# A new hand-over list of steps for a one-core kernel that mixes an S5 scan and a Hedgehog linear attention

## The chip, the core and the metric

One core of a Trainium2 chip. Engines with a queue of instructions each: PE (TensorE, matrix products into PSUM), PEld (its weight loads), DVE (VectorE), ACT (ScalarE), POOL (GpSimd), and SP (SyncE), which here only issues DMAs. The metric is the device time of one execution in microseconds, lower is better.

## The reference, cut to what matters

`x` is 2048 x 512, bfloat16. Branch A is a diagonal complex state-space scan over the 2048 positions with 512 states; branch B is linear attention with 32 heads of width 16, whose features are softmaxes of a small projection and of its negative. A gate per position mixes them.

```python
g = sigmoid((x * gate_w).sum(-1, keepdims=True))
# A: h[t] = Lam_bar * h[t-1] + x[t] @ B_bar.T ; a = 2 * Re(h @ C.T) + x * Dskip
# B: q, k, v = heads of x @ wqkv; phi(u) = [softmax(u @ w_phi), softmax(-u @ w_phi)]
#    b = (phi(q) @ (phi(k).T @ v)) / (phi(q) @ phi(k).sum(0) + 1e-6) @ wo
out = g * a + (1 - g) * b
```

## The kernel before, in words

Positions are cut into 16 tiles of 128 rows. In the scan's layout row `c*8 + r` belongs to residue `r`, so tiles `2r` and `2r+1` hold residue `r`. The work is a set of generators, one for each piece; each `next` of a generator is one step and emits a few instructions for one or two engines. The string `ORDER` names the steps one after the other, and this order is the order of the instructions in the queues of PE, DVE, ACT and SP: nothing is reordered later, and only semaphores hold an instruction back. In a token, `@b` gives the PSUM banks that the step opens (eight banks, 0 to 7), `:D` puts a copy out of PSUM (or an absolute value) on DVE instead of ACT, `:A` issues an output DMA from ACT instead of SP, and `F:n` emits n matrix products whose result nobody reads. A bank is free again when its copy out of PSUM is done.

Before the list, SP issues `w_phi`, the transposing loads of x tiles 0 to 3 (line 229), the 512 KB of `Wv`, and x tiles 4 to 7; ACT issues the two halves of the k weights (line 165). The steps that the text speaks of:

- `NR`, `NI` (line 284): loads of the two 512 KB halves, real and imaginary, of A's matrix B; `l8` to `l15`: x tiles 8 to 15; `R0` to `R7` (line 288): transposes of B on the DMA queue, which wait for both halves; `Q`, `C`, `J`: loads for q's weights and A's matrix C; `O` (line 305): the 512 KB of `wo`. All are issued by SP.
- `W0` to `W3` (PE transposes of the k weights, line 274, then a copy), `f0` to `f3` (products that fold `w_phi` into them, line 431, then a copy; `fj` needs `Wj`), `V`, `P`, `P2`, `P3`, `P4`, `U`, `i0` to `i3`, `M`, `D`: scalars and tables of the scan; `M` runs on POOL, and `D` on DVE needs it. `L` pins an ACT table.
- `k0` to `k15`, `v0` to `v15`, `q0` to `q15` (line 475): four products of 512 columns and a copy out of PSUM. `kn` and `vn` need x tile n.
- For each group of k tiles (2, 2, 4, 4, 4 of them) `x` and `n` (maximum, minimum, line 511, then the differences, lines 521 and 527, DVE), `e` (exponentials, ACT), `s` (sums, DVE; logarithm, ACT; last a product, line 548, DVE) and `a` (the kv sums, PE, lines 578 and 582, into two banks held to the end; step `Y` reads them out, and `G` makes the gate). For the four groups of q tiles the same work is `xA`, `nA`, `eA`, `sA` and `X`, `N`, `E`, `S` with 1 to 3; there the last product (line 559) is followed by four DMA transposes (line 563) into `phT`, one per tile.
- `g` with r and j (lines 601 to 608): input of residue r for two of the eight state tiles, with a copy; `z0` to `z3`: the scan on DVE (line 641); `h` with r and j (line 668): states of the other residues, twenty of them added up on DVE (line 672); `c0` to `c7` (lines 590 and 594): scaled C matrices, with scratch space in `phT` of the first q group.
- For each output tile n: `y` (line 717, states times C, 512 columns; line 722, the skip term), `o` (line 736: numerator and denominator in two halves, on ACT a logarithm and a copy each, then an exponential; line 744 a product on DVE; then a DMA transpose, line 758, or for n = 12 to 15 a PE transpose, line 753, and a copy), `t` (line 765: times `wo`, onto y's bank; line 769 or 771 the gate; line 773 the output DMA). `o` of tile n needs transpose n of its group.

The list was written by a planner outside of the kernel that holds costs and landing times; of it the kernel has only the list.

Of the kernel before, what the change touches and what calls it, by code (L numbers as in the profile page):

```python
# [20 lines left out]
P = 128  # L21
MAGIC = 12582912.0
Z_MAX = 70.0
ORDER = """
B F:28 l11 F:4 W1@0 W0@1 W2@2 W1:D f1@3 W3@4 f1 W0:D f0@5 f0 NR W2:D f2@6 W3:D f3@0 f3 f2:D V@1 V P P P P2 P2 P2 P2 P2
P4 U P3 P4 P4 i1 i2 U l12 i1 i2 U F:4 k0@2 k0 NI P2 P3 l10 i0 l9 k1@3 k1 x0 i1 i1 i0 i2 k3@4 l14 x0 k2@5 n0 U M i1 k2
V2@6 v3@1 i2 x0 i0 v0@7 i0:D i0 v2@0 x0 k3 l8 n0 l13 i3 x0 k5@2 k5 i3 k4@3 v0 R0 x1 k6@5 n0 n0 i3 i3:D x1 x1 i2 k4 n0
v1@4 i3 L V2 k7@2 k7 n1 n1 x1 n1 gw x1 n1 R1 v6@7 e0 e0 v1 k6:D v4@6 n1 x2 n2 v7@3 v7 k11@2 v6 s0 x2 s0 e1 n2 s0 v5@5
v5 s0 s0 R2 D k12@4 R3 k10@3 k9@7 v4 k8@5 n2 l15 s0 e1 k13@6 v2 s1 k10 k14@0 s0 k11 C1 Q2 k8 C4 g20@3 s1 x2 k13 a0@25
k14 a0 n2 s1 k12 g20 x2 g00@6 k9 g30@0 s1 s1 s1 x2 n2 s1 v3 g40@4 x3 g01@3 g10@7 n3 R5 g00 a1 a1 x3 g60@1 n3 e2 R4  # L30
g11@6 g10 x3 g01 n3 e2 x3 e2 e2 n3 g11 k15@3 g60 g10 g30 g40 x3 s2 n3 g70@1 k15 g11 s2 x4 s2 s2 n4 g30 Q1 Q3 x4 n4 e3
e3 x4 C5 n4 Q0 x4 g50@7 g50 g50 s2 g21@4 n4 g21 s2 s2 v8@3 e3 e3 s3 g70 g70 g70 z0 s3 z0 g31@6 g31 s3 z0 z0 v11@0
g41@7 a2 C6 a2 g41 z0 z0 v11 g61@4 a2 g61 C7 w0@1 w0 C3 w1@7 w1 g31 a2 w2@0 w2 w3@4 s3 s3 g51@1 g51 g51 z0 R7 z0 x4
g62@7 w3 z0 z0 g71@6 g71 g02@0 v8 n4 s3 J2 g71 g71 z1 g02 z1 h50@1 h50 J2 z1 e4 e4 q1@4 h10@3 g62 g12@6 h10 g22@0 q2@1
z1 z1 z1 g22 q2 s3 z1 z1 q1 e4 h60@3 h60 g12 g12 z1 q3@7 q0@0 q0 q3 g32@1 e4 xA C2 g42@4 g32 nA g32 s4 g42 v9@6 v9 z1
s4 C0 J0 J0 g52@0 g52 c4 g52 nA c4 xA c4 R6 g72@7 g72 J1 s4 nA g23@3 g43@1 g03@4 g63@6 g72 g72 z2 h51@0 J3 c5 a3 g23
z2 J1 v10@7 h11@3 nA a3 c2 c2 g03 xA z2 z2 z2 z2 c0 h51 h61@4 z2 z2 g13@0 v10 xA h11 g43 c3 g13 a3 a3 J3 c5 z2 s4
g33@7 g13 g33 c0 z2 s4 s4 g33 h32@1 c2 h32 xA g53@3 g63 h52@0 g53 g53 nA s4 h52 h42@7 h42 eA c5 eA v14@1 v14 g73@6 g73
g73 q5@3 g73 h61 h12@0 h12 v12@1 v15@7 z3 z3 c0 z3 v12 eA eA h21@4 z3 v13@6 h21 a4 z3 z3 sA v13 z3 z3 c3 q10@0 q10
q6@1 v15 sA c1 c1 q4@4 q4 q6 a4 a4 c3 a4 h20@6 h30@0 h30 c7 q8@7 q12@4 q8 Y Y sA z3 z3 h33@2 q5 sA sA c1 h62@1 h20  # L40
h02@0 h33 sA sA q7@7 h62 G h43@3 h53@6 h02 c7 h13@2 Y Y sA q7 y6@1 h13 h01@0 h53 q12 c7 sA sA c6 q14@5 q14 h23@7 h23
h22@4 h31@2 h00@6 c6 q13@5 h31 h41@7 h43 c6 h22 h40@3 h63@2 h00 h41 h63 h40 h03@6 h03 sA sA y3@4 y3 END X1 o0@7 N1 X1
q13 o0 o0@2 O o0 N1 X1 q9@6 q9 N1 o1@3 X1 o1 o1@5 q11@7 o0 N1 X1 N1 o3@2 o1 o3 q11 X2 o1 o1 h01 X2 N2 X2 o3@6 o3 N2 X2
N2 E1 E1 E1 o1 E1 o0 o0 X2 S1 S1 N2 y0@3 o2@5 y0 y0 o2 o2@2 y3 o2 o2 y1@7 y1 S1 o3 o3 o3 S1 G y2@0 N2 q15@6 q15 S1 S1
o2 y1 o2 t1 S1 S1 G G y9@5 y9 E2 E2 y4@2 y4 y2 N3 E2 E2 y5@6 y9 y5 t1 S1 S1 S1 S1 X3 t3 t3 y2 t2 t2 X3 N3 N3 S2 X3 S2
t0 o4@7 y5 o4 o4@4 o4 N3 o4 X3 S2 y4 t0 y13@0 S2 o4 o5@7 o5 o5@4 o5 o5 y6 o4 y6 o6@3 S2 o6 o6@7 o6 X3 o5 y7@4 y7 o5 S2
S2 o7@3 N3 y13 o6 t4 t0:A o6 o6 E3 E3 E3 S2 S2 y8@7 t4:D o7:D E3 S3 t5 S2 S2 S2 t5 y12@2 S3 S3 o7@3 o7 o7 o7 t6 t6
o8@6 o8 o8@3 o8 o7 y12 y8 S3 t1:A o8 o8 o9@1 o9 o9@6 o8 y11@3 y11 S3 S3 y10@1 o9 o9 o9 S3 S3 t4:A o11@6 y7 t7 y12 o9
o11 t7 o10@6 y8 t8 t8 y11 y13 o11@4 t9 S3 S3 S3 o10 o11 S3 o10@7 t9:D y15@6 y14@4 o11 o11 o10 o10 t8:A o12@7 o12 o12@5
o12:D y15 o10 o12 o12 o11 o13@7 o13 o13@5 o13 o13 t2 y14 y14 o10 o12@7 t7:A t5:A o12:D o14@5 o14:D t3:A y10 o15@7 t9:A  # L50
y10 o15 o15@5 o15:D o15 o13 t12 o15 o14@7 o14 o14 t12:D t12 t11 t11:D o15@5 o15 o13@7 t10 t6:A t11 y15 o13:D t10 t10
t15 t15 t15:A o14 o14@2 t13 o14:D t13 t13 t14 t14 t14:A
"""
H_VECTOR = tuple((r, j) for r in (1, 2, 4, 5, 6) for j in range(4))
OT_PE = (12, 13, 14, 15)
# [792 lines left out]
```

## Time and profile before

| what | us |
|---|---|
| median of 3 runs (lowest to highest) | 156.41 (155.97 to 156.71) |
| the profiled execution | 156.63 |
| its span in the profile | 154.6 |
| busy PE, DVE, ACT, POOL | 147.7, 131.8, 129.4, 16.1 |
| first product on PE, last product's group begins | 1.11, 149.11 |
| queue q1 (SP's DMAs), share of 16 DMA engines | 53.2% of the span |

All times below count from the start of the span. A row in order of time gives start, length, engine, line, operation, result and operands, and the number of instructions merged; the bracket gives the idle time before it and what ended that. In rows of SP the length is that of issuing, and a separate view gives the time from issue to landing.

### The profile page before, as it was taken

How to read it: one execution, taken by the hardware profiler on the slowest of the kernel's cores; microseconds unless marked ns; L12 is line 12 of the kernel's file. 1: busy time of each engine (PE TensorE's matmuls, PEld its weight loads, DVE VectorE, ACT ScalarE, POOL GpSimd, SP SyncE). 2: the span in 40 equal slices, each digit the busy share in tenths (PEclk: the TensorE clock that was granted, in tenths of full speed). 3: DMA queues.
4: the chain of work that ended last, by engine and by line, in shares of the span. 5: the costliest groups of instructions: out<-in, count | busy, mean ns of one | idle time of the engine just before them, and what ended most of it. 6: DMA issues, size and time to landing. Idle time of an engine off the chain costs nothing.

```text
span 154.6 us, 3382 instructions
## 1 busy us (share of the span) xinstructions
PE 147.7 (96%) x1254; PEld 95.6 (62%) x1254; DVE 131.8 (85%) x303; ACT 129.4 (84%) x279; POOL 16.1 (10%) x43
## 2 busy tenths in 40 slices
PE   7999999999999999999999999999998999989990
PEld 7844444797789876888755767454454545545540
DVE  3789999999999999999999999999997966423730
ACT  3489999999999999999999996799497998465652
POOL 8239980000000000000000000000000000000000
PEclk9999999999999999999999999999999999999999
DMA  4785998465475849910000006943169689789742
GB/s 120 158 222 87 168 191 170 89 98 107 97 78 105 174 94 168 184 25 6 0 0 4 0 0 136 141 136 68 34 123 143 117 163 197 150 137 200 208 147 94
DMA packets 50848, 17.55 MB, mean 113 GB/s; under 512 B 44176, under 2 KB 50832, under 8 KB 50832
## 3 DMA queue, kind: packets, MB, share of 16 engines
q1 hardware_dynamic: 48544, 15.36, 53.2%
q10 hardware_dynamic: 2128, 1.97, 4.5%
q8 instruction: 10, 0.16, 0.4%
q14 instruction: 6, 0.05, 0.1%
q0 software_dynamic: 160, 0.01, 0.1%
HBM read 2.64 MB, written 2.10 MB: 31 GB/s over the span
## 4 chain that ended last, share of the span: by engine, by line
DVE 47%; PE 32%; DMA 8%; ACT 6%; issue 4%; DVEq 0%; SPq 0%
PE py L717 9%; DVE smk L511 6%; PE pk L475 6%; DMA oT<-on 5%; PE py L765 5%; PE pgq L601 4%; DMA phT<-EEq 3%; DVE Bn L672 3%; DVE EEk L548 3%; DVE w L641 3%; DVE HM L672 3%; DVE H L652 3%; PE spin L812 3%; DVE EEk L527 2%; DVE EEk L521 2%
## 5 line engine op out<-in xcount | busy, mean ns | idle before, releaser
L601 PE MATMUL pgq<-xT,BT 128*128 128x256 bf16 x256 | 31.2, 272 | 0.0
L475 PEld LDWEIGHTS <-xT 128*128 128x128 bf16 x192 | 18.3, 98 | 18.6 <-DMA xT<-in_A_x_dram 0.8
L601 PEld LDWEIGHTS <-BT 128*128 128x128 bf16 x256 | 24.7, 98 | 3.9
L138 ACT ACTIVATE EEk<-EEk 128x1024 bf16<-128x1024 bf16 x20 | 20.6, 1075 | 0.3 <-DVE EEk L527 0.3
L765 PE MATMUL py<-Wo,oT 128*128 128x512 bf16 x64 | 16.1, 379 | 0.9 <-DMA oT<-on 0.9
L119 ACT CAST uv<-pgq 128x512 bf16<-128x512 f32 x28 | 16.3, 604 | 0.3
L475 PE MATMUL pq<-Wq,xT 128*128 128x512 bf16 x64 | 15.8, 379 | 0.0
L475 PE MATMUL pv<-Wv,xT 128*128 128x512 bf16 x64 | 15.6, 379 | 0.0
L475 PE MATMUL pk<-Wk,xT 128*128 128x512 bf16 x64 | 15.0, 379 | 0.3 <-ACT EEk L138 0.3
L138 ACT ACTIVATE ld<-pn 128x16 f32<-128x16 f32 x32 | 6.2, 193 | 7.6 <-PE pn L736 7.4
L138 ACT ACTIVATE EEq<-EEq 128x1024 bf16<-128x1024 bf16 x12 | 11.8, 1061 | 0.3 <-DVE EEq L527 0.3
L590 ACT ACTIVATE phT<-X,dgB 128x512 bf16<-128x512 bf16 x16 | 11.5, 740 | 0.0
L769 ACT ACTIVATE ot<-py,G 128x512 bf16<-128x512 f32 x12 | 8.0, 684 | 3.5 <-PE py L765 3.3
L119 ACT CAST nu<-pn 128x256 bf16<-128x256 f32 x28 | 10.3, 381 | 0.0
L736 PEld LDWEIGHTS <-phT 128*128 128x128 bf16 x128 | 6.7, 98 | 5.3 <-DMA phT<-EEq 1.2
L765 PEld LDWEIGHTS <-oT 128*128 128x128 bf16 x64 | 5.6, 97 | 6.2 <-DMA oT<-on 1.2
L119 ACT CAST vx<-pv 128x512 bf16<-128x512 f32 x16 | 9.4, 600 | 0.0
L548 DVE TENSOR_TENSOR EEk<-EEk,rck 128x4096 bf16<-128x4096 bf16 (+1 forms) x5 | 9.3, 1859 | 0.0
L119 ACT CAST Xq<-pq 128x512 bf16<-128x512 f32 x16 | 9.1, 610 | 0.2
L736 PE MATMUL pn<-KVm,phT 128*128 128x68 bf16 x128 | 8.0, 194 | 0.8 <-DMA phT<-EEq 0.7
L119 ACT CAST Xq<-pk 128x512 bf16<-128x512 f32 x15 | 8.4, 618 | 0.4 <-PE pk L475 0.4
L511 DVE TENSOR_TENSOR smk<-smk 128x512 bf16<-128x512 bf16 (+4 forms) x18 | 8.6, 476 | 0.1
(177 smaller groups left out, 319.6 us busy)
## 6 DMA issues: line engine op xcount, KB each, us to landing
X<-HM SPq DMA_DIRECT2D x8, 256.0 KB, 4.0
out_dram<-ot ACTq DMA_DIRECT2D x11, 128.0 KB, 2.5
out_dram<-ot SPq DMA_DIRECT2D x5, 128.0 KB, 2.5
C2r<-in_B_wqkv_dram ACTq DMA_DIRECT2D x2, 256.0 KB, 3.3
Wv<-in_B_wqkv_dram SPq DMA_DIRECT2D x1, 512.0 KB, 4.0
Bn<-in_A_B_re_dram SPq DMA_DIRECT2D x1, 512.0 KB, 5.5
Bn<-in_A_B_im_dram SPq DMA_DIRECT2D x1, 512.0 KB, 6.7
Wo<-in_B_wo_dram SPq DMA_DIRECT2D x1, 512.0 KB, 4.6
```

What stands on the lines that cost most here:

```text
L119: nc.scalar.copy(out=out_ap, in_=in_ap)
L138: ins = nc.scalar.activation(**kw)
L475: MM(out=pt[:], lhsT=xT[:, kt, ti * P:(ti + 1) * P], rhs=W[:, kt, :], start=(kt == 0), stop=(kt == KT - 1))
L511: VT(out=dst, in0=cur[:, :, :, 0:n, :], in1=cur[:, :, :, n:2 * n, :], op=op)
L548: VT(out=E5, in0=E5, in1=rc.to_broadcast([P, L, 2 * NB, Dh, 4]), op=ALU.mult)
L590: nc.scalar.mul(out=t_, in_=x_, mul=c_)
L601: MM(out=pg[:, h, :], lhsT=BT[:, kt, 2 * j + h, :], rhs=xT[:, kt, r * NC:(r + 1) * NC], start=(h == 0 and kt == 0), stop=(r % 2 == 0 and k ...
L672: VT(out=dst, in0=ph[:], in1=uv[j][:, r], op=ALU.add)
L717: MM(out=py[:], lhsT=hs(r, t, slice(a * P, (a + 1) * P)), rhs=C2B[t], start=(t == 0), stop=False)
L736: MM(out=pn[:, 4 * m:4 * m + 4, :].rearrange("p h e -> p (h e)"), lhsT=ph[:, 4 * hf + m, :], rhs=KVm[:, 4 * hf + m, :], start=(m == 0), st ...
L765: MM(out=py[:], lhsT=oT[:, g, :], rhs=Wo[:, g, :], start=False, stop=(g == HG - 1))
L769: nc.scalar.mul(out=ot[:], in_=py[:], mul=G[:, ti:ti + 1])
```

## The change

The string `ORDER` is replaced; nothing else is touched. Both lists have 855 tokens and the same steps. Their order and banks differ, and so do some marks: `W0` and `W3` are copied by ACT instead of DVE, `f1` by DVE instead of ACT; `i2` and `i3` change engines for the absolute value; `o7`, `o9`, `o11`, `o12`, `o15`, `t7`, `t10`, `t11`, `t12` and `o13` differ in some copies, and outputs go 8 times through ACT instead of 11. `NR` and `NI` now stand first, ahead of all of `l8` to `l15`; before, `l11` stood ahead of both and `l12` between them. Two groups of four fills moved from before `W1` and before `k0` to behind `V` and `f3`. The sums use banks 7 and 1 instead of 2 and 5. The diff, cut:

```diff
 ORDER = """
-B F:28 l11 F:4 W1@0 W0@1 W2@2 W1:D f1@3 W3@4 f1 W0:D f0@5 f0 NR W2:D f2@6 W3:D f3@0 f3 f2:D V@1 V P P P P2 P2 P2 P2 P2
-P4 U P3 P4 P4 i1 i2 U l12 i1 i2 U F:4 k0@2 k0 NI P2 P3 l10 i0 l9 k1@3 k1 x0 i1 i1 i0 i2 k3@4 l14 x0 k2@5 n0 U M i1 k2
-V2@6 v3@1 i2 x0 i0 v0@7 i0:D i0 v2@0 x0 k3 l8 n0 l13 i3 x0 k5@2 k5 i3 k4@3 v0 R0 x1 k6@5 n0 n0 i3 i3:D x1 x1 i2 k4 n0
-v1@4 i3 L V2 k7@2 k7 n1 n1 x1 n1 gw x1 n1 R1 v6@7 e0 e0 v1 k6:D v4@6 n1 x2 n2 v7@3 v7 k11@2 v6 s0 x2 s0 e1 n2 s0 v5@5
-v5 s0 s0 R2 D k12@4 R3 k10@3 k9@7 v4 k8@5 n2 l15 s0 e1 k13@6 v2 s1 k10 k14@0 s0 k11 C1 Q2 k8 C4 g20@3 s1 x2 k13 a0@25
...
-h02@0 h33 sA sA q7@7 h62 G h43@3 h53@6 h02 c7 h13@2 Y Y sA q7 y6@1 h13 h01@0 h53 q12 c7 sA sA c6 q14@5 q14 h23@7 h23
-h22@4 h31@2 h00@6 c6 q13@5 h31 h41@7 h43 c6 h22 h40@3 h63@2 h00 h41 h63 h40 h03@6 h03 sA sA y3@4 y3 END X1 o0@7 N1 X1
-q13 o0 o0@2 O o0 N1 X1 q9@6 q9 N1 o1@3 X1 o1 o1@5 q11@7 o0 N1 X1 N1 o3@2 o1 o3 q11 X2 o1 o1 h01 X2 N2 X2 o3@6 o3 N2 X2
...
-o2 y1 o2 t1 S1 S1 G G y9@5 y9 E2 E2 y4@2 y4 y2 N3 E2 E2 y5@6 y9 y5 t1 S1 S1 S1 S1 X3 t3 t3 y2 t2 t2 X3 N3 N3 S2 X3 S2
-t0 o4@7 y5 o4 o4@4 o4 N3 o4 X3 S2 y4 t0 y13@0 S2 o4 o5@7 o5 o5@4 o5 o5 y6 o4 y6 o6@3 S2 o6 o6@7 o6 X3 o5 y7@4 y7 o5 S2
-S2 o7@3 N3 y13 o6 t4 t0:A o6 o6 E3 E3 E3 S2 S2 y8@7 t4:D o7:D E3 S3 t5 S2 S2 S2 t5 y12@2 S3 S3 o7@3 o7 o7 o7 t6 t6
-o8@6 o8 o8@3 o8 o7 y12 y8 S3 t1:A o8 o8 o9@1 o9 o9@6 o8 y11@3 y11 S3 S3 y10@1 o9 o9 o9 S3 S3 t4:A o11@6 y7 t7 y12 o9
-o11 t7 o10@6 y8 t8 t8 y11 y13 o11@4 t9 S3 S3 S3 o10 o11 S3 o10@7 t9:D y15@6 y14@4 o11 o11 o10 o10 t8:A o12@7 o12 o12@5
-o12:D y15 o10 o12 o12 o11 o13@7 o13 o13@5 o13 o13 t2 y14 y14 o10 o12@7 t7:A t5:A o12:D o14@5 o14:D t3:A y10 o15@7 t9:A
-y10 o15 o15@5 o15:D o15 o13 t12 o15 o14@7 o14 o14 t12:D t12 t11 t11:D o15@5 o15 o13@7 t10 t6:A t11 y15 o13:D t10 t10
-t15 t15 t15:A o14 o14@2 t13 o14:D t13 t13 t14 t14 t14:A
+NR F:28 NI B W1@0 W0@1 W0 W2@2 W1:D W3@3 W3 f1@4 W2:D f0@5 f2@6 f0 f1:D l10 V@0 F:4 V P f3@1 f3 f2:D F:4 P P k1@2 k1
+l13 P2 k0@3 P2 U P2 P2 P2 P2 P4 k2@4 P3 P3 k3@5 P4 P4 k0 v0@0 i0 i2 U i0 i0 i1 i2 k4@7 i0:D i0 k2 i2 i2:D i2 U k3 k5@6
+i1 v3@1 n0 x0 l9 i1 V2@2 i3 l12 x0 k4 v2@3 i3 i3 l14 i1 k5 n0 x0 n0 x0 i3 k7@4 n0 x0 U n0 i1 l11 k6@5 n1 x1 x1 n1 x1
+n1 l8 R0 R1 x1 i3 k7 M v7@7 x1 n1 n1 k6:D L V2 v1@6 x2 n2 e0 v6@4 v5@5 v4@2 e0 x2 s0 v0 l15 n2 s0 n2 v2 s0 v1 R2 s0 v6
+v3 n2 k10@0 k10 s0 k9@3 k9 C4 k13@6 gw D R3 s0 k12@4 e1 v7 s0 e1 s1 C6 k11@1 k11 x2 s1 k14@0 k8@3 k12 k14 k8 v4 k13
...
+n4 Q3 n4 s2 g50 g21@6 e3 s3 v8@0 g31@2 g11 Q2 g11 n4 g70@3 Q1 s3 C7 g21 g70 v9@5 g70 g70 z0 z0 g31 g31 Q0 w1@6 C0 a2
+a2 a2 w0@3 s3 z0 v11@2 v9 g61@5 g41 R4 z0 w1 v8 z0 z0 g61 s3 w2@4 s3 s3 a2 x4 z0 z0 g51@6 g51 x4 w2 C2 s3 w3@0 g51 v11
...
+q8@6 q5@7 h62@3 h41@5 c3 h41 c1 c3 c3 h13@0 h62 q11@2 h13 q11 q8 q12@1 c6 q12 h21@5 q5 h21 h02@2 c7 q4@6 q4 h53@3 h53
+h23@1 h23 h33@0 h33 sA q9 h40@7 h40 sA q7@5 h43@6 h63@3 c7 h43 q7 c7 y4@0 y4 sA h63 sA h03@1 END h02 o0@4 o0 X1 N1
+o1@7 o1 q14@6 X1 N1 h03 o0@5 X1 o1@2 o1 o1 o0 o0 q15@3 o2@4 o2 o2@7 o2 N1 q15 X1 N1 X1 N1 E1 E1 y2@1 y1@2 y1 E1 E1 q14
...
+S1 y1 E2 E2 E2 E2 y9@6 G N3 y5 y5 y3@4 y2 X3 X3 N3 t1 G t1 N3 S1 N3 S2 y9 y9 S2 S2 S1 S1 S2 y3 y3 t3 y0 t0 t0 t2 t2
+y6@7 X3 t2:A o4@2 o4 o4@5 o4 o4 y6 y6 t3 X3 o4 X3 o4 S2 S2 t3 o5@1 o5 o5@2 o5 o5 y13@5 y13 o5 N3 o6@4 S2 o6 o6@1 o6 o6
+y12@2 o5 y7@4 y7 y12 o6 o6 t4 y7 S2 S2 t4:D S2 E3 E3 E3 E3 S2 o7@1 o7 t5 t5 S3 o7@0 o7 S3 o7 t6 S3 o7 S2 o7 y8@1 o8@3
+t6 o8 o8@0 o8 o8 S3 S3 y12 t0:A y11@7 o8 o8 o9@3 o9:D o9@0 o9:D S3 y8 y8 o9 o9 S3 S3 o9 o10@3 y11 o10 o10@0 y11 o10
+o10 S3 y14@3 S3 y14 t7 t7:D t8 y14 t8 y15@0 o11@4 S3 o11 o11@1 t9 o12@4 o11:D o11 S3 o10 o10 o12 o12@1 o12 o12 t9:D
+o11 y15 o13@4 o13:D o13@6 t6:A o13 o13 o11 o12 y10@1 o14@4 y15 o14:D o12@6 t9 o12:D t7:A t1 y10 y10 o13 o15@4 o15
+o15@6 t4:A t5 o15 o15 t8 o15 t12 t12 t12:A t10 o14@4 o14 o14 t10:D o13@6 t11 o15@2 o15 t10 o13:D t11 t11:A y13 t13 o14
+o14@1 t15 t15 t15 o14:D t14 t13 t13 t14 t14:A
 """
```

More of the change, by code (lines that the diff above doesn't have):

```diff
@@ L30 @@
[L30 to L39, printed above, removed]
@@ L40 @@
-q6@1 v15 sA c1 c1 q4@4 q4 q6 a4 a4 c3 a4 h20@6 h30@0 h30 c7 q8@7 q12@4 q8 Y Y sA z3 z3 h33@2 q5 sA sA c1 h62@1 h20
-h02@0 h33 sA sA q7@7 h62 G h43@3 h53@6 h02 c7 h13@2 Y Y sA q7 y6@1 h13 h01@0 h53 q12 c7 sA sA c6 q14@5 q14 h23@7 h23
-h22@4 h31@2 h00@6 c6 q13@5 h31 h41@7 h43 c6 h22 h40@3 h63@2 h00 h41 h63 h40 h03@6 h03 sA sA y3@4 y3 END X1 o0@7 N1 X1
-q13 o0 o0@2 O o0 N1 X1 q9@6 q9 N1 o1@3 X1 o1 o1@5 q11@7 o0 N1 X1 N1 o3@2 o1 o3 q11 X2 o1 o1 h01 X2 N2 X2 o3@6 o3 N2 X2
-N2 E1 E1 E1 o1 E1 o0 o0 X2 S1 S1 N2 y0@3 o2@5 y0 y0 o2 o2@2 y3 o2 o2 y1@7 y1 S1 o3 o3 o3 S1 G y2@0 N2 q15@6 q15 S1 S1
@@ new lines @@
+i1 v3@1 n0 x0 l9 i1 V2@2 i3 l12 x0 k4 v2@3 i3 i3 l14 i1 k5 n0 x0 n0 x0 i3 k7@4 n0 x0 U n0 i1 l11 k6@5 n1 x1 x1 n1 x1
+n1 l8 R0 R1 x1 i3 k7 M v7@7 x1 n1 n1 k6:D L V2 v1@6 x2 n2 e0 v6@4 v5@5 v4@2 e0 x2 s0 v0 l15 n2 s0 n2 v2 s0 v1 R2 s0 v6
+v3 n2 k10@0 k10 s0 k9@3 k9 C4 k13@6 gw D R3 s0 k12@4 e1 v7 s0 e1 s1 C6 k11@1 k11 x2 s1 k14@0 k8@3 k12 k14 k8 v4 k13
+a0@71 a0 x2 s1 x2 s1 v5 g00@4 g00 g60@0 n2 x3 s1 g20@3 g60 s1 g10@2 g10 n3 e2 g30@6 g40@5 g10 s1 a1 x3 g20 n3 a1 x3 n3
+x3 g41@4 n3 C3 e2 e2 e2 x3 g30 g40 g30 k15@0 k15 n3 e3 s2 x4 s2 x4 g01@2 g01 e3 e3 s2 g50@3 g11@5 g50 s2 s2 s2 n4 x4
@@ new lines @@
+n4 Q3 n4 s2 g50 g21@6 e3 s3 v8@0 g31@2 g11 Q2 g11 n4 g70@3 Q1 s3 C7 g21 g70 v9@5 g70 g70 z0 z0 g31 g31 Q0 w1@6 C0 a2
+a2 a2 w0@3 s3 z0 v11@2 v9 g61@5 g41 R4 z0 w1 v8 z0 z0 g61 s3 w2@4 s3 s3 a2 x4 z0 z0 g51@6 g51 x4 w2 C2 s3 w3@0 g51 v11
+n4 R5 w3 g71@5 g71 g71 g71 z1 z1 g02@4 g02 g42@6 a3 a3 z0 z0 g42 w0 e4 e4 z1 z1 z1 g62@2 g12@0 q1@5 C1 h50@4 C5 J1 e4
+e4 z1 q2@6 q2 g12 g12 g22@3 g22 J0 h50 z1 z1 g62 q3@4 q3 J2 s4 z1 s4 q0@6 z1 s4 q0 q1 xA nA g32@0 J3 g32 g32 h60@3 J0
+g52@2 g52 c4 h60 J2 c4 g52 h51@4 c2 s4 s4 g72@6 R7 g72 xA h10@5 nA g72 g72 c2 xA J3 nA h10 v10@0 v10 J1 s4 c5 h51 c5
@@ new lines @@
+R6 g23@3 v12@2 c4 c0 c0 g63@5 nA z2 z2 a3 a3 g03@4 xA g03 z2 z2 z2 z2 xA g23 z2 z2 g33@6 c5 v12 z2 z2 g13@0 g13 g63
+g43@4 h32@3 g13 nA g43 h52@2 h52 g33 h32 h61@5 h61 h12@0 c0 g53@4 h12 g33 g53 s4 v14@3 c2 eA eA h42@2 h42 g73@6 g53 eA
+eA g73 g73 q10@5 sA h11@0 h11 O h00@4 g73 sA v13@2 h00 v13 a4 z3 sA v15@6 z3 v15 h20@0 h01@4 h30@2 v14 h20 sA h30 z3
+h31@6 z3 z3 sA a4 h01 h31 c6 c6 sA q13@3 q13 z3 a4 a4 Y Y h22@0 G q10 z3 z3 G q6@2 q6 h22 z3 z3 sA sA Y Y c1 c1 q9@4
+q8@6 q5@7 h62@3 h41@5 c3 h41 c1 c3 c3 h13@0 h62 q11@2 h13 q11 q8 q12@1 c6 q12 h21@5 q5 h21 h02@2 c7 q4@6 q4 h53@3 h53
@@ new lines @@
+h23@1 h23 h33@0 h33 sA q9 h40@7 h40 sA q7@5 h43@6 h63@3 c7 h43 q7 c7 y4@0 y4 sA h63 sA h03@1 END h02 o0@4 o0 X1 N1
+o1@7 o1 q14@6 X1 N1 h03 o0@5 X1 o1@2 o1 o1 o0 o0 q15@3 o2@4 o2 o2@7 o2 N1 q15 X1 N1 X1 N1 E1 E1 y2@1 y1@2 y1 E1 E1 q14
+X2 y0@5 y0 o1 y4 X2 N2 X2 o0 o0 o3@4 o3 o3@7 o3 o1 o3 y2 X2 N2 o2 X2 N2 S1 S1 N2 S1 o3 S1 N2 S1 S1 o3 y5@3 o2 o2 S1 S1
+S1 y1 E2 E2 E2 E2 y9@6 G N3 y5 y5 y3@4 y2 X3 X3 N3 t1 G t1 N3 S1 N3 S2 y9 y9 S2 S2 S1 S1 S2 y3 y3 t3 y0 t0 t0 t2 t2
+y6@7 X3 t2:A o4@2 o4 o4@5 o4 o4 y6 y6 t3 X3 o4 X3 o4 S2 S2 t3 o5@1 o5 o5@2 o5 o5 y13@5 y13 o5 N3 o6@4 S2 o6 o6@1 o6 o6
```

## The prediction, with its working

> **What bounds the kernel now.** I read the page's busy line first, then the table by stage, then PE, SP and DVE in order of time. The busy line, and of the table the three stretches from 24 to 96 us (columns: length, then busy time of PE, PEld, DVE, ACT, POOL, then clock, DMA share, GB/s):
>
> ```profile
> PE 147.7 (96%) x1254; PEld 95.6 (62%) x1254; DVE 131.8 (85%) x303; ACT 129.4 (84%) x279; POOL 16.1 (10%) x43
> ```
> ```profile
> 24.00:48.00 24.00, 24.00 (x258) 18.80 (x257) 23.93 (x44) 23.55 (x45) 0.00 (x0) 1.00 0.58 104
> 48.00:72.00 24.00, 24.00 (x238) 19.37 (x235) 23.78 (x54) 23.48 (x45) 0.00 (x0) 1.00 0.59 112
> 72.00:96.00 24.00, 24.00 (x216) 16.15 (x213) 23.80 (x49) 22.93 (x43) 0.00 (x0) 1.00 0.09 21
> ```
>
> The reader is to see three engines full at once. A busy PE need not be PE at its peak, so I took start-to-start paces from the PE timeline: 0.216 us for 512 columns, 0.109 for 256, 0.056 for 128, 0.032 for the 68 columns of pn, 0.030 for those of the kv sums, 0.107 for a fill. Times the counts: k, v, q, t 256 x 0.216 = 55.3; y 128 x 0.216 + 64 x 0.056 = 31.2; g and h 384 x 0.109 = 41.9; sums 192 x 0.030 = 5.8; pn 128 x 0.032 = 4.1; 64 small ones x 0.056 = 3.6; 36 fills 3.9. That is 145.7 us. PE starts at 1.12 and ends its last matmul near 150.8: only **4.1 us** of its path is waiting, and no order of the steps can give more than that. Its waits in the PE timeline (bracket: idle time and what ended it):
>
> ```profile
> 23.69 4.49 PE L475 MATMUL pk<-Wk,xT 128*128 128x512 bf16 x20 [0.31 <-ACT EEk L138]
> ...
> 117.94 0.30 PE L736 MATMUL pn<-KVm,phT 128*128 128x68 bf16 x4 [0.73 <-DMA phT<-EEq]
> ...
> 137.07 1.04 PE L765 MATMUL py<-Wo,oT 128*128 128x512 bf16 x4 [0.57 <-DMA oT<-on]
> ...
> 146.93 1.04 PE L765 MATMUL py<-Wo,oT 128*128 128x512 bf16 x4 [0.31 <-DMA oT<-on]
> ```
>
> By start-to-start the losses are 0.44 up to the first fold, 0.73 more up to 23.7 (0.47 of it k10 waiting for its x tile: the weight loads show 0.8 on that landing, so the name ACT is the later event only), 0.44 up to 101, 0.96 at o4, 0.81 up to t9, 0.70 after it. DVE sets when o4 can start: its full queue reaches S1's last multiply at 111.77, and the first transpose behind it lands at 113.06 + 4.8 = 117.9. The same chain comes again for S3 (SP and DVE rows):
>
> ```profile
> 7.22 7.13 SPq L229 DMA_TRANSPOSE xT<-in_A_x_dram  x5
> 14.40 0.74 SPq L284 DMA_DIRECT2D Bn<-in_A_B_re_dram  x1
> 15.19 1.30 SPq L229 DMA_TRANSPOSE xT<-in_A_x_dram  x1
> 16.53 0.59 SPq L284 DMA_DIRECT2D Bn<-in_A_B_im_dram  x1
> 17.17 6.93 SPq L229 DMA_TRANSPOSE xT<-in_A_x_dram  x5
> 24.21 5.13 SPq L288 DMA_TRANSPOSE BT<-Bn  x4
> ...
> 134.30 6.69 SPq L563 DMA_TRANSPOSE phT<-EEq  x4
> ```
> ```profile
> 111.77 1.23 DVE L559 TENSOR_TENSOR EEq<-EEq,rhoq 128x2048 bf16<-128x2048 bf16 x1
> ...
> 132.37 1.22 DVE L559 TENSOR_TENSOR EEq<-EEq,rhoq 128x2048 bf16<-128x2048 bf16 x1
> ```
>
> **How I compare the lists.** Both have the same steps, so no engine's sum changes but by the marks :D and :A: ACT +0.2 us, DVE +0.3, three outputs move from ACT's queue to SP's. For each step I add up the paces of the work ahead of it on its engine in the old and the new list. Where that sum is reached in the trace gives a clock for the new place; the waits are then argued one by one.
>
> **Start.** Four fills fewer stand ahead of W1: 4 x 0.107 = 0.43 earlier, at 4.1, when the first half of its matrix (issued 0.79, 3.3 to landing) is just there. W0's and W3's copies go to ACT (0.59 each, against 0.42 on DVE), so f0 waits to about 5.9 and f3 to 6.3; the eight fills now stand between these. k1 starts near 7.3, as k0 did at 7.46, with 6.87 ahead: loss 0.4 (0.3 to 0.9). DVE is rid of two copies (0.34 each) and its first P step comes near 7.2, not 7.95; ACT's first sine about 0.3 earlier. POOL's chain of M, which ended at 22.06, starts with that sine and still ends before D (22.4 ahead on DVE, it ran at 23.9), which waits for it.
>
> **x tiles behind both halves of B.** On SP five tiles took 7.13 us; the fifth was l11. Now both halves follow x7: issues near 12.4 and 13.1, then l10 at 13.8, l13, l9, l12, l14, l11, l8 at 1.3 each to 22.9; R0 at 22.9, 1.3 sooner. Landings by the issue view: B's halves 5.5 and 6.7 us after issue (19.9, 23.2), l12 between them at 20.5, l10 6.5 (23.7), l9 24.0: in order of issue, B_im taking 2.7 behind l12. So now B_re 17.9, B_im 20.6 to 21.2, l10 21.1 to 21.7, each next tile 0.4 to 0.7 later. k10 has 20.79 ahead and comes at 21.2: waits 0 to 0.5, k9 about as much at 22.1. I take 0.35, and 0.25 for the other small losses there: **0.6** (0.25 to 1.2), where 0.73 was. [...] The landings above came in order, so I keep 0.35.
>
> **Middle, 24 to 113.** PE waited nearly nowhere. In the new list 11 places on PE come before the ACT copy that frees their bank or feeds them, by clocks: v9 0.73 before g11's copy (PE 44.3), g70 0.63, g72 0.52, y4's second half 0.42 before c7 (on DVE), v11 0.40, and six of 0.2 to 0.35, 4.2 in all. A delay for one delays all behind it and so covers the others, and ACT comes some 0.3 to 0.7 sooner from the start. I take 0.5 for the stretch to 96 (0 to 0.7; 4.2 if they add), and 0.4 at y4 (0 to 0.7): c7's add moved from 91.4 to 94.6 us of DVE work. s and z steps stay: S1's last multiply has 109.15 ahead, not 109.23; S2's and S3's 118.88 and 124.98, not 118.95 and 124.71. The Wo load, which stood behind sA's four transposes at 99.19, now goes ahead of them into SP's idle time after 62; t1, its first user, has 110.8 ahead: free. sA's last transpose waits for c7 (near 97.3), lands near 101; o3, which waited 0.28 for it, now has 103.9 ahead.
>
> **o4.** PE has 115.81 ahead, not 115.37 (0.44 more work before the wait). Losses so far 0.4 + 0.6 + 0.5 + 0.4 = 1.9: PE is there at 117.7; the transpose lands at 117.9, or up to 0.6 sooner if DVE keeps its early lead. Loss to here **2.0**, where it was 2.57.
>
> **Tail.** t9 stood 4.1 us behind o9's issue; now t9 has 135.54 ahead, at 137.6, and o9 is issued near 132.5: lands by 136.5, its 0.81 goes. What is late next is S3: PE reaches o12 at 138.4, o13 139.5, o14 140.6, with 8.1 us of PE work from o14 on (7.7 before). SP passes S2's four transposes, o7, o8, o9 at 1.3 each and gives S3's from 133.5 on (134.30). S3's landed 3.6, 3.3, 4.7, 3.9 after issue, the third at 142.6, where o14 followed at 142.68. New third issue 135.9 to 137.2, landing 139.6 to 141.9: o14 waits 0 to 1.4; I take **0.6**. o10's transpose goes behind all four, near 140, lands 143.8; t10 has 141.41 ahead, 144.0 with the losses: 0.2 (0 to 0.5). Small ones 0.25. Outputs on SP stand behind the last o transpose and hold up nothing; after the last matmul 3.8 us follow as before. Tail 1.05, where it was 1.51.
>
> **Sum.** Losses 2.0 + 1.05 = 3.05, not 4.08: 1.0 us less. The profiled execution took 156.63 us (span 154.6 and 2.0 around it): 155.6; the median of the runs is 0.22 lower, 156.41, so on their scale **155.4**. Of this kernel some 0.5% (0.8 us) can be told from no change: faster is below 155.6, slower above 157.2.
>
> **Rivals.**
> - *S3's landing eats the rest.* Third transpose as late as 141.9 and t10 late too: 0.8 + 0.3 more. For it: 4.7 us and a 2.14 us issue in S3, both unlucky in the trace; against: S2's third took 3.7. Near 156.4, no change. Chance 0.2.
> - *The ACT waits add up* (slower). ACT was full 98% of 24 to 72; if each copy is late afresh, 4.2 takes the place of 0.9: 155.4 + 3.3 = 158.7 in full, near 157.8 if two in three add. It decides when PE comes to o4 later than 119 or so, some 1.1 behind the landing. Against: ACT's lead, and PE's own delay, which lets ACT catch up. Chance 0.23.
> - [...] The fill pace was 0.107 until 5.03, then half. Fewer fills and eight transposes fill that time now; if the step came one such stretch (3.9 us) later, PE's 2 to 3 us of work there would take twice as long, less the idle 0.5: near 157.4. [...] Chance 0.05.
> - *The early lead lasts* on DVE and ACT, l10 is in time: losses 1.7, 154.1. Chance 0.05.
>
> **Numbers.** Forecast 0.47, own range 154.7 to 156.1 (0.42 faster, 0.05 same). Faster 0.42 + 0.05 = 0.47; same 0.05 + 0.2 = 0.25; slower 0.28. Range: 154.2 to 158.0, which leaves out the ends of the cases on both sides.
>
> **What would show it.** Right: k1 near 7.3; k10 near 21.5; R0 issued near 23; PE without idle over 0.5 from 24 to 96; o4 at 117.3 to 117.9; t9 without a wait; o14 waiting for phT near 141. Wrong: PE waiting for ACT copies again and again from 40 to 70; x tiles landing after 23; S1's multiply later than 112; S3's transposes issued after 134.3.

## The result, and the profile after

The changed kernel took **155.21 us** (median of 6 runs, 154.92 to 155.6), the kernel before 156.56 beside it: ratio **0.9916, 95% interval 0.9887 to 0.9944**. Measured once more it was 0.9926 (0.9896 to 0.9956). The profiled execution took 155.28 us, its span is 153.2. So it is faster by 0.8%, near the 155.4 forecast. The path to that number was in good part another one than the prediction's. Medians below are of all runs of a kernel while ratios leave out slow executions, and a traced execution can lie over 1 us from its kernel's median (the repeat of the changed kernel: 156.77 against 155.55), so a trace tells where that one execution lost its time.

The page's busy line and its chain by engine (18 of the 1254 matmul records are missing, the weight loads are complete):

```profile
PE 146.2 (95%) x1236; PEld 95.0 (62%) x1254; DVE 132.4 (86%) x303; ACT 129.2 (84%) x279; POOL 15.8 (10%) x43
...
PE 78%; SPq 10%; DMA 7%; issue 1%; ACT 1%
```

PE in order of time, where it waited, and where it waited before (o4, t9):

```profile
6.90 0.16 PE L310 MATMUL pvt<-ident,vec_n 12*128 12x12 bf16 x1 [0.29 <-DMA vec_n<-in_A_log_dt_dram]
...
22.89 1.25 PE L475 MATMUL pk<-Wk,xT 128*128 128x512 bf16 x5 [0.16 <-DMA xT<-in_A_x_dram]
...
117.46 0.43 PE L736 MATMUL pn<-KVm,phT 128*128 128x68 bf16 x8
...
121.13 0.43 PE L736 MATMUL pn<-KVm,phT 128*128 128x68 bf16 x8 [0.18 <-DMA phT<-EEq]
...
137.60 1.02 PE L765 MATMUL py<-Wo,oT 128*128 128x512 bf16 x4
```

The waits of 0.73 at o4 and 0.57 at t9 are gone; what is left are small ones at the start, at an x tile, and a new one at o6. With start-to-start paces as in the prediction PE loses 2.00 us (1.49 up to o4, 0.51 after it), where it lost 3.83 (2.42 and 1.41; the prediction, with rounder clocks, has 4.08). Its last product starts at 148.79, not 150.62. Of these 1.83 us the end gives 0.4 back. SP and DVE:

```profile
12.36 1.28 SPq L284 DMA_DIRECT2D Bn<-in_A_B_re_dram  x1
13.69 0.62 SPq L284 DMA_DIRECT2D Bn<-in_A_B_im_dram  x1
14.36 9.97 SPq L229 DMA_TRANSPOSE xT<-in_A_x_dram  x7
24.38 1.26 SPq L288 DMA_TRANSPOSE BT<-Bn  x1
...
113.03 6.66 SPq L563 DMA_TRANSPOSE phT<-EEq  x4
...
134.83 5.39 SPq L563 DMA_TRANSPOSE phT<-EEq  x4
```
```profile
111.75 1.22 DVE L559 TENSOR_TENSOR EEq<-EEq,rhoq 128x2048 bf16<-128x2048 bf16 x1
...
132.00 1.23 DVE L559 TENSOR_TENSOR EEq<-EEq,rhoq 128x2048 bf16<-128x2048 bf16 x1
```

The reader is to see that DVE's S1 (111.75) and SP's first transpose behind it (113.03) have not moved: 111.77 and 113.06 before. Four transposes take 5.39 us to issue in one place and 6.66 in the other. That difference became the key.

### The profile page after: what moved, and what is told of

The parts are those of the page before. It is cut to its first block, busy times and chain, and to the rows that moved or that the text cites. A ratio compares the mean times of both kernels' runs of the same rounds, so it can differ in the third digit from the quotient of the medians.

```text
span 153.2 us, 3361 instructions
## 1 busy us (share of the span) xinstructions
PE 146.2 (95%) x1236; PEld 95.0 (62%) x1254; DVE 132.4 (86%) x303; ACT 129.2 (84%) x279; POOL 15.8 (10%) x43
## 4 chain that ended last, share of the span: by engine, by line
PE 78%; SPq 10%; DMA 7%; issue 1%; ACT 1%
PE pgq L601 18%; PE py L717 16%; PE pq L475 9%; PE py L765 8%; SPq L229 8%; PE pv L475 4%; PE ph L668 4%; PE pk L475 4%; DMA xT<-in_A_x_dram 4%; PE kvacc L578 3%; DMA phT<-EEq 3%; PE pn L736 3%; PE pgq L606 2%; PE py L722 2%; PE pgq L608 2%; SPq L284 1%
## 5 line engine op out<-in xcount | busy, mean ns | idle before, releaser
L765 PE MATMUL py<-Wo,oT 128*128 128x512 bf16 x62 | 15.3, 379 | 0.1
L590 ACT ACTIVATE phT<-X,dgB 128x512 bf16<-128x512 bf16 x16 | 10.7, 725 | 0.0
L744 DVE TENSOR_TENSOR on<-nu,rd 128x512 bf16<-128x512 bf16 x16 | 6.7, 421 | 2.8 <-ACT rd L138 1.6
L736 PEld LDWEIGHTS <-phT 128*128 128x128 bf16 x128 | 6.2, 97 | 3.8 <-DMA phT<-EEq 1.4
L511 DVE TENSOR_TENSOR smk<-smk 128x512 bf16<-128x512 bf16 (+4 forms) x18 | 8.1, 448 | 0.1
```

The lines of the kernel that those rows point to most:

```text
L511: VT(out=dst, in0=cur[:, :, :, 0:n, :], in1=cur[:, :, :, n:2 * n, :], op=op)
L590: nc.scalar.mul(out=t_, in_=x_, mul=c_)
L736: MM(out=pn[:, 4 * m:4 * m + 4, :].rearrange("p h e -> p (h e)"), lhsT=ph[:, 4 * hf + m, :], rhs=KVm[:, 4 * hf + m, :], start=(m == 0), st ...
L765: MM(out=py[:], lhsT=oT[:, g, :], rhs=Wo[:, g, :], start=False, stop=(g == HG - 1))
```

## The experiments

Twelve runs, each of five rounds. The expectations call their theories by letters: L (PE waits at o4 for S1's landing, whatever it gains ahead of that), F (the gain is made in the front), T (in the tail), C (the packets described below), K (DVE and ACT follow PE). Against the kernel before beside them (156.7 to 156.95 us):

| kernel | median us | ratio (95%) |
|---|---|---|
| new front, old tail | 156.50 | 0.997 (0.995 to 0.9991) |
| old front, new tail | 156.83 | 1.0012 (0.9987 to 1.0037) |
| before, 16 fills | 156.88 | 0.9994 (0.9975 to 1.0014) |
| changed, 16 fills | 156.49 | 0.9976 (0.9956 to 0.9996) |
| changed, again | 155.55 | 0.9926 (0.9896 to 0.9956) |
| changed, short fills | 158.25 | 1.007 (1.0035 to 1.0105) |
| before, short fills | 156.83 | 1.0002 (0.9981 to 1.0023) |
| changed, t13 first | 155.69 | 0.9919 (0.9887 to 0.9951) |
| changed, NI later | 155.56 | 0.9923 (0.9897 to 0.9948) |
| changed, q split | 155.82 | 0.993 (0.9902 to 0.9957) |
| changed, all three | 155.31 | 0.9897 (0.9868 to 0.9927) |
| before, q split | 155.28 | 0.9903 (0.9874 to 0.9931) |

**Which half of the list?** Both lists have nearly the same steps done when o4 begins, so I cut there: the first 679 tokens of one list, then what is left in the order of the other, with its banks renamed to fit.

> The new list up to the first step of o4, then the old list's order of what is left (banks renamed so that they fit). Theory L (o4 starts when the first q transpose of the second group lands, and what PE gains ahead of that is lost in the wait there; the tail decides half of the gain): o4 at 117.4 to 117.5, then the old tail with its waits before t9 and t10 (0.7 and 0.5): about 0.8 us less than before, 155.7 where before is 156.5. Rival F (the gain is made ahead of o4, in the start and at the x tiles, and goes through to the end): like after, 155.2. Rival T (only the tail's order counts): like before, 156.5.

> The old list up to o4, then the new list's order of what is left. Theory L: o4 at 117.4 to 117.9 behind the landing, no wait at t9 and t10 after it, the three output copies in a row on ACT at the end: about 155.7. Rival F: like before, 156.5. Rival T: like after, 155.2.

Measured: -0.3% and +0.1%; neither half carries the gain alone. PE with the new front and the old tail:

```profile
117.39 0.42 PE L736 MATMUL pn<-KVm,phT 128*128 128x68 bf16 x8
...
118.70 0.29 PE L736 MATMUL pn<-KVm,phT 128*128 128x68 bf16 x4
119.57 0.29 PE L736 MATMUL pn<-KVm,phT 128*128 128x68 bf16 x4 [0.58 <-ACT ot L769]
...
121.00 0.43 PE L736 MATMUL pn<-KVm,phT 128*128 128x68 bf16 x8
```

o4 is early, as in the changed kernel; by the paces 1.15 us is lost at o5 and o6 and 1.3 at t8, t9 and t11. In the other hybrid PE came to o4 at 118.99, behind a transpose that landed 4.8 us after its issue. Its S1 was 1.0 us later than in the kernel before, though the list is the same up to there; DVE was 0.5 us behind from 9 us on, which is how much two executions of the same steps can differ. F falls with the first kernel, T with the second, and L, which wanted 0.8 us from both, with the second too.

**Is there a cushion at o4?** 16 fills near 28 us, into a bank that is free there.

```diff
-... x2 g00@6 k9 ...
+... x2 F@6:16 g00@6 k9 ...
         if tok == "F":
+            if banks:
+                spin = bank([P, 512], F32, "spin2")
```

> The kernel before with 16 fills (128 columns, 16 x 0.056 = 0.9 us of PE work) ahead of the first product of g00, near 28 us. Theory L: PE had 0.90 us of waiting at o4, so nothing comes out at the end: 0 to +0.2 us. Rival F: +0.9 us. Third (the three engines are so closely coupled between 24 and 96 us that a late PE makes ACT and DVE late too, and S1 with them): +0.5 to +0.9, with the first transpose of the second group issued later than 113.06.

> The changed kernel with the same 16 fills ahead of g00. Theory L: no cushion is left at o4, so PE comes 0.9 later there; the wait of 0.35 at o6 and 0.1 at o13 fall away: +0.4 to +0.6 us. Rival F: +0.9. Third (coupled engines): +0.9 or more, with S1's transposes issued later too.

Measured: nothing, and 0.8 us against the changed kernel's repeat. The first looks like L, but the traces say otherwise. The kernel before with fills, on DVE, on SP, and the time of its first transpose from issue to landing:

```profile
113.17 1.22 DVE L559 TENSOR_TENSOR EEq<-EEq,rhoq 128x2048 bf16<-128x2048 bf16 x1
```
```profile
114.58 5.39 SPq L563 DMA_TRANSPOSE phT<-EEq  x4
```
```profile
phT<-EEq SPq DMA_TRANSPOSE x1, 3.2
```

S1 came 1.4 us later than in the kernel before (0.3 of it from the start, the rest with the fills and behind them): DVE follows PE between 30 and 45 us, and L's fixed landing is wrong. In the changed kernel with fills S1's first transpose was issued at 115.25 instead of 113.03, so there the third expectation, coupled engines, is nearest. But the transpose then landed 3.2 us after its issue, where it took 4.8 in the kernel before and 4.4 in the changed one. That paid for the fills.

**What makes a transpose slow?** In the kernel before, the first of S1's transposes (window 113.0 to 113.2) and what the DMA queues carried from 115 to 117:

```profile
phT<-EEq SPq DMA_TRANSPOSE x1, 4.8
```
```profile
q8 instruction: 1, 0.02, 4.0%
```

One 16 KB packet of kind "instruction" started at 115.65 and kept one DMA engine for 1.28 us. Ten of them come in each trace (0.16 MB on q8 in the whole of the kernel before), 114 to 151 of PE's products apart, 128 in the mean (kernel before). That the count of PE's products sets when they come is my estimate from that spacing. The transposes beside the packets pay: over the first ten traces (from 90 us on) those into `phT` landed 3.3 us after issue where no instruction packet ran meanwhile (114 of them), and 4.3 where one of q8 did (37; nine more met only a packet of another queue, q14); 12 of those 37 also took over 1.45 us to issue (4 of the 114). Theory C follows: where the packets fall decides who waits. It was tested by moving them, with no order changed. First, every fill cut into two of half the width:

```diff
-            for _ in range(int(eng)):
-                MM(out=spin[:, 0:P], lhsT=fillw[:], rhs=fillw[:], start=True, stop=True)
+            for _ in range(2 * int(eng)):
+                MM(out=spin[:, 0:64], lhsT=fillw[:], rhs=fillw[:, 0:64], start=True, stop=True)
```

> The changed kernel as it is, as a base for the three beside it, on the same chip. Expected from its first result: 0.992 of before (0.9887 to 0.9944), S1's second transpose issued for 2.2 us again, since a 16 KB packet of the queue q8 (kind: instruction) ran at 114.0 to 115.5 then.

> The changed kernel with every fill cut into two of half the width (64 columns), so the same PE time but 36 products more ahead of the rest; the ten 16 KB packets of q8 have come every 128 products or so, and should come 36 products earlier in the work: from 114.0 to about 108.5 us, and from 132.4 to about 128.3, out of S1's and S3's transposes. Theory C (such a packet holds up the transposes that it meets by about 1 us, in issue or in landing, and it lay in S1's and S3's in both kernels): all of S1's and S3's issues 1.2 to 1.3 us, no wait at o6 (0.35), S3's first issue at 133.9 to 134.1 instead of 134.8: -0.3 to -0.6 us against c1. Rival (long issues and late landings come by chance or from the queue's own load): the same as c1, long issues still between 113 and 118.

> The kernel before with the same halving of its 36 fills. Theory C: the packet of 115.65 comes near 109, S1's first transpose lands 3.9 us after issue instead of 4.8, so that the wait of 0.90 at o4 shrinks to 0.1 or less; the packet of 135.0 comes near 131.4 and S3's issues are all 1.3 us; the waits at t9 and t10 stay: -0.6 to -1.0 us against before, which would make most of what the change brought a matter of where these packets fall. Rival (chance): the same as before. Second rival (the packets play a part, but the S1 chain on DVE sets o4): -0.2 to 0.

The packets moved (114.06 to 109.85 in the changed kernel, 115.65 to 109.18 in the one before), and S1's transposes ran clean: 5.4 us for four, the first landing after 3.2; no wait at o4 or o6. Yet the kernel before gained nothing and the changed one lost 2.3 us by the ratios. The first packet had moved too, from 12.3 to about 8, among the x tiles and `Wv`: k3 waited 0.71 for its x tile in one, v0 0.60 for `Wv` in the other; later packets met o7 (t7: 0.96) and o10 (t10: 1.50). These waits are not worked out to the whole of the 2.3. So the fills were the wrong handle, and the next pair left the first 58 us alone: q products of 512 columns cut into two of 256, which by the paces is as much PE time (2 x 0.109 us for 0.216) and 24 products more.

```diff
-        tile_mm(pq, order[n], Wq2)
+        if n in (0, 1, 2, 3, 5, 10):
+            ti = order[n]
+            for c in (slice(0, 256), slice(256, 512)):
+                for kt in range(KT):
+                    MM(out=pq[:, c], lhsT=xT[:, kt, ti * P:(ti + 1) * P], rhs=Wq2[:, kt, c], ...)
+        else:
+            tile_mm(pq, order[n], Wq2)
```

> The kernel before with six q tiles cut in halves (q0 to q3, q5, q10), 24 products more, nothing ahead of 58 us changed. Theory C: the packet of 115.65 comes near 111.5, ahead of S1's transposes; the first lands 3.2 us after issue instead of 4.8, at 116.3, before PE comes to o4 at 117.0: the wait of 0.9 there goes. The packet of 135.0 comes near 132.5 and meets o8, o9 or S3's first. In full -0.9 us, and -0.3 to -0.9 with what it meets later; about half or more of what the change brought would then be where the packets fell. Rival (the waits come again at t7 to t10 as in the run with short fills): 0.

> The changed kernel with the products of six q tiles (q0 to q3, q10, q13) cut into two halves of 256 columns: the same PE time, 24 products more, from 60 us on. Nothing ahead of 60 us changes. Theory C: the 16 KB packets of q8 that came at 114.0 and 132.4 come near 110.5 and 129.5; S1's first transpose lands 3.2 us after issue instead of 4.4, all of S1's issues take 1.3, the wait at o6 goes: -0.2 to -0.4 us against the changed kernel, 0.990 of before. Rival: the packets always meet something that is needed, and what is won at o6 is lost at t7 to t11: 0.

The kernel before with split q: **0.9903**, as much as the whole change brings. Its DVE and SP, its first transpose, and PE at o4 (lines are 6 higher here):

```profile
111.72 1.22 DVE L565 TENSOR_TENSOR EEq<-EEq,rhoq 128x2048 bf16<-128x2048 bf16 x1
```
```profile
113.16 5.39 SPq L569 DMA_TRANSPOSE phT<-EEq  x4
```
```profile
phT<-EEq SPq DMA_TRANSPOSE x1, 3.2
```
```profile
116.81 0.29 PE L742 MATMUL pn<-KVm,phT 128*128 128x68 bf16 x4
```

Its six runs lie between 155.19 and 155.68, all 20 of the kernel before between 156.24 and 158.01. Up to S1 it is the kernel before within 0.1 us. The packet ran at 109.88, the transpose landed 1.5 us sooner, the wait at o4 is gone, and so is the one of 0.28 at o3 (packet from 97.69 to 94.89). In the tail the packet now at 130.46 cost 0.94 at o11, where t9 and t10 had cost 1.2. In all PE loses 2.35 instead of 3.83. The changed kernel with split q gained nothing: its wait at o6 went, t7 waited 0.63 for o7's transpose (5.0 us to landing, a packet at 131.4), as C's rival had it. But its traced execution (155.94) had lost 0.7 us long before the first q product, which the edit cannot have done:

```profile
5.72 1.03 PE L274 MATMUL ptw<-ident,C2r 128*128 128x128 bf16 x8 [0.37 <-DMA C2r<-in_B_wqkv_dram]
```

The second half of the k weights landed at 5.67 (5.13 in the changed kernel's trace), products of 128 columns started every 0.107 us until 7.07 and every 0.056 only then (4.93 there), k1 began at 8.35 instead of 7.67, and DVE was 0.7 us later from 9 us on, so that S1's multiply came at 112.47. The step from 0.107 to 0.056 comes between 4.4 and 7.1 us in the fourteen traces, early and late under both lists: at 5.03 in the kernel before, and at 6.72 with the old front and the new tail. So this run doesn't show what clean transposes in S1 are worth to the new list.

**The x tiles.** NI behind l10, l9 and l13:

```diff
-NR F:28 NI B ... l10 ... l13 ... l9 ... l12 l14 l11 l8 R0
+NR F:28 B ... l10 ... l9 ... l13 NI ... l12 l14 l11 l8 R0
```

> The changed kernel with the load NI put behind l10, l9 and l13 on SP instead of ahead of all x tiles; nothing else. The wait for x tiles at k10 and k9 (0.33 us in the first trace, 0.7 and 0.8 in the two later ones) should go; R0 should stay near 24.4, since SP's queue sets it. Theory K (DVE and ACT follow PE closely from 30 to 45 us, as the fills showed, so S1 comes earlier too): S1's last multiply near 111.3, 0.3 to 0.6 us less than the changed kernel (0.989 of before). Theory L (S1 on DVE stays at 111.75, and PE waits for it at o4 instead): 0 to -0.1 us (0.992 of before).

The changed kernel, then this one, on PE from 21.7 us:

```profile
22.89 5.35 PE L475 MATMUL pk<-Wk,xT 128*128 128x512 bf16 x24 [0.16 <-DMA xT<-in_A_x_dram]
28.21 0.43 PE L578 MATMUL kvacc<-vx,EEk 128*128 128x68 bf16 x8
```
```profile
21.75 6.21 PE L475 MATMUL pk<-Wk,xT 128*128 128x512 bf16 x28
28.31 0.43 PE L578 MATMUL kvacc<-vx,EEk 128*128 128x68 bf16 x8 [0.36 <-DVE EEk L548]
```

All 28 products run through without a wait, and PE then stands at a0 for DVE's product of the first k group (line 548). a0 starts no sooner, and S1's multiply comes at 111.83. (Up to 119 us DVE is within 0.15 us of the changed kernel's trace; what this trace lost, 1.6 us, is at t7.) By time: 0.9923, the same as the changed kernel. So the wait for an x tile costs nothing as long as a0 is next: neither K nor L's reason (o4), but L's number.

**The end.** t13's copy ahead of t15's:

```diff
-y13 t13 o14 o14@1 t15 t15 t15 o14:D t14 t13 t13 t14 t14:A
+y13 t13 o14 o14@1 t15 t13 t13 t15 t15 o14:D t14 t14 t14:A
```

> The changed kernel with t13's output copy ahead of t15's on ACT at the end; there ACT waited 1.00 us for t15's product while t13's was there, and then made three copies in a row of 0.62 us each. If the longer end of the changed kernel (4.4 us after the last product's group begins instead of 4.0) comes from that order: -0.3 us against c1. Rival (the output DMA's issue or landing sets the end): 0.

ACT at the end, in the changed kernel and in this one:

```profile
148.34 1.84 ACT L769 ACTIVATE ot<-py,G 128x512 bf16<-128x512 f32 x3 [1.00 <-PE py L765]
```
```profile
147.67 1.27 ACT L769 ACTIVATE ot<-py,G 128x512 bf16<-128x512 f32 x2 [0.42 <-PE po L753]
149.12 0.69 ACT L769 ACTIVATE ot<-py,G 128x512 bf16<-128x512 f32 x1 [0.18 <-PE py L765]
```

From the start of t14's product to its copy on ACT 1.07 us instead of 1.36: the 0.3 is there in the trace. The runs (0.9919 against 0.9926) cannot tell it.

> The changed kernel with the three edits together: NI behind three x tiles, the six q tiles cut in halves, t13's output copy ahead of t15's. If K and C hold: 0.4 + 0.3 + 0.3 = 1.0 us less than the changed kernel, 0.986 of before. If L holds with C: 0.3 to 0.6 less, 0.989. If none of the waits was what held the end: 0.992.

0.9897 (0.9868 to 0.9927): 0.45 us below the changed kernel's repeat, with intervals that overlap. It is clearly faster than the kernel before; that it beats the changed kernel is not shown.

## Why the prediction was right, and where it was not

- *Start, 0.4 expected, 0.8 measured at k1.* W1 came at 4.54, not 4.1: it waited 0.47 for the first half of its matrix, which landed 3.7 us after issue and not 3.3. In the other eight traces that begin with the new front W1 came between 4.08 and 4.32, so 4.1 was nearly right and this trace had a late landing. V waited for `log_dt`. The rival of a later step in PE's pace did not come true in this trace: 128-column products go from 0.107 to 0.056 us at 4.93, against 5.03 before. In others the step came up to 2 us later; what sets its time was not tested. DVE and ACT had no early lead: P's second step at 7.78, not 7.2, and the first x step 0.9 later than before.
- *x tiles, 0.6 with the small losses, 0.43 measured.* The landings were as worked out: 18.1 and 20.5 for B, l10 at 21.0, all in order of issue, and k9 waited 0.33. R0 was wrong (24.38, not 22.9): seven tiles and NR took 11.3 us to issue. The step that failed is that this wait was priced at all. DVE sets a0 at 28.2 behind it. What the change is named after is worth nothing at the end in the changed kernel.
- *Middle 0.5 and y4 0.4; 0.27 and 0 measured.* No wait from 34 us to o4. The rival of adding ACT waits is out.
- *o4, 2.0 expected, 1.49 measured, at 117.46 within the range given.* The number held for a wrong reason. I took the landing of 4.8 us as the transpose's own. It is 3.2, and 1.6 came from the instruction packet; undisturbed it would have landed at 116.3 by estimate (113.06 + 3.2), before PE came at 117.0. In the new list the packet runs at 114.0 instead of 115.65, the landing takes 4.4, and PE has 0.44 us more work ahead, so it comes at the moment of the landing.
- *Tail, 1.05 expected, 0.51 measured.* t9 as forecast; o14 and t10 hardly wait. S3's first transpose was issued at 134.83, not 133.5 (after 134.3, which the prediction named as a sign of being wrong), since o9's issue ahead of it took 1.98 us (a packet at 132.44), and S3's transposes then landed in 3.2 to 3.3. Not foreseen: o6, 0.35, behind S1's second transpose that took 2.25 us to issue (the packet at 114.0), and 0.4 at the end for three copies in a row. In the repeat of the changed kernel the packet at 132.4 met o7's transpose (5.6 us to landing), and t7 waited for it, so the tail's 0.5 was a good draw. PE there:

```profile
135.93 0.82 PE L765 MATMUL py<-Wo,oT 128*128 128x512 bf16 x3 [1.27 <-DMA oT<-on]
```
- *The sum.* Losses of 2.00 instead of 3.05 are 1.05 less than forecast. The 0.4 at the end, which no term had, and the 0.25 by which the old losses were taken too high give most of that back, so the profiled 155.28 lies 0.3 under the 155.6 forecast for it. That the number came so close is luck in part.
- *What the gain is.* About 1.5 us of the old list's waits went when its packets moved and no step did. The new list has a packet in S1 as well, but at o4 it costs nothing. Without a packet in S1 the two lists were not shown to differ (0.9903 against 0.993, and 0.9897 with all three edits; the intervals overlap). What each would take with no packets at all was not measured, so how much of the 0.8% is the order's own stays open.

## What to carry to other kernels

Before a late landing is taken as a transfer's own time, look for what else ran on the DMA engines meanwhile, and compare it with the same transfer elsewhere in the trace. A wait that the trace shows is worth its length only if the next wait behind it is not already due: take it away on its own and see. Where a list of steps beats another by a per cent, a control that keeps the order and shifts only the count of instructions tells luck from order. Before two traces are compared behind an edit, compare them ahead of it: what differs there is not the edit's.

## What the runs showed of the hardware

An instruction packet of 16 KB took 0.9 to 1.8 us on one DMA engine (140 of them in fourteen traces). A transpose into `phT` in flight with it landed 4.3 us after issue in the mean instead of 3.3. Of the 55 transposes that SP issued within half a us of such a packet's start 53 took 1.5 to 2.9 us to issue instead of 1.25, which delayed what stood behind it on SP's queue (four of S1's took 6.66 us to issue instead of 5.39); long issues occurred without a packet too (2.08 at 18.33 in the changed kernel). Adding 24 products of no extra PE time (two of 0.109 us for one of 0.216) moved the packets by 1 to 6 us and the kernel before by 1.5 us. The pace of PE's products doubled (0.107 us to 0.056 for 128 columns) 4.4 to 7.1 us after the start, differently in executions of the same first steps.
